# Decay tables by powers on GpSimd instead of exponentials on ScalarE, in a fused retention and gated feed-forward kernel

## The chip, the cores and the metric

The kernel runs on one core of a Trainium2 chip. The core has a matrix engine (TensorE, "PE" in the profile, with its weight loads as "PEld"), VectorE ("DVE"), ScalarE ("ACT"), GpSimd ("POOL"), a sync engine that issues most of the DMAs ("SP"), and 16 DMA engines. Every engine works through its own queue in order; semaphores make one engine wait for another. The metric is the device time of one execution in microseconds; the table below gives three runs of it. Times inside the kernel are counted from the start of the profiled span.

## What is computed

The inputs q, k and v have 8 batches, 8 heads, 576 positions and 64 values a head. Each head has a decay factor, and each score is weighted by the decay to the power of the distance:

```python
scores = (1.0 / np.sqrt(D_)) * np.matmul(q, k.transpose(0, 1, 3, 2))
gamma = 1.0 - 2.0 ** (-5.0 - np.arange(H, dtype=np.float32))
rel = pos[:, None] - pos[None, :]
Dmat = np.where(rel >= 0, gamma[:, None, None] ** rel[None, :, :], 0.0)
attn = np.matmul(scores * Dmat, v)
x = attn.transpose(0, 2, 1, 3).reshape(B * S, H * D)       # 4608 x 512
out = (sigmoid(x @ w_gate) * (x @ w_val)) @ w_out          # d_ff = 1536
```

There is no softmax, so the weight gamma to the power (i - j) can be split: q at position i is multiplied by gamma to the power i, and k (or v) at position j by gamma to the power -j. The kernel does so with two small tables, `qtab` (which also holds the scale of one over the root of 64) and `ktab`.

## The kernel before, in words

All of the work is written out in one program order, and each engine's queue follows that order; nothing reorders it at run time.

The first 512 positions of batch 0 and the first 256 of batch 1 are taken in three "pairs" of 256 positions (`load_pair`, `cast_pair`); everything else in "steps" of 128 positions (`load`, `cast_qk`, `cast_v`). For a pair, q, k and v arrive in f32 in six pieces. A piece of k is multiplied by the table `ktab2` on GpSimd (`kp`, L412), a piece of q by `qtab2` on VectorE (`qp`, L412); v is only cast to bf16 on GpSimd (`vp`, L409). TensorE then transposes kp and qp (`kTp`, `qTp`, L466), ScalarE copies the transposes out of PSUM (`kT`, `qT`, L476), TensorE computes scores (`qkp`, L485), VectorE multiplies them with the causal mask `trip` (`ptp`, L492), and TensorE multiplies them with v (`pvp`, L600) and sums up states (`st`, L522). Between these small groups the program puts matmuls on zeros (`fill`, L242, tile `idle`), ten at the very start and ten more between the first transposes and scores.

The outcome, transposed, is `xT`, and the feed-forward part takes it from there: gate and value matmuls (`hg`, `hv`, L1343 and L1408 for the first 512 rows, L885 and L1015 for later blocks), Sigmoid on ScalarE, a product on VectorE or GpSimd, and the output matmuls (`op`, L1502 and L1275). The weights arrive in f32 too, and are cast to bf16 in pieces (`cast_w`, L309), the first ones on GpSimd behind the kp and vp of the first two pairs. The loads of q, k, v of the first pairs and of the weights are all issued by the sync engine in one order (two half pieces by ScalarE), into 18 landing buffers (twelve called "ld" and six called "gsum"), which are used again in turn, so that the nineteenth load needs the first buffer free.

The decay tables are made at the very start, by `tables`, which is called twice: for the pairs with a tile of 128 x 2 x 8 x 2 (32 columns), and for the steps with one of 128 x 5 x 8 x 1 (40 columns). Each call makes an iota of positions `pos` on GpSimd (L252), multiplies it by the logarithm of each head's decay into `arg` (eight small VectorE instructions, L260), and takes two exponentials on ScalarE (L261 and L262). Between the calls stands the identity for the transposes (GpSimd, masks.py); the second call also corrects the positions of the last chunk on VectorE (L273). Then come a warm-up Sigmoid on ScalarE (L279), four VectorE memsets `sbd` (L285), and the mask `trip` on GpSimd (L288 and L290). Only behind these stand the first kp on GpSimd and the first qp on VectorE. Exp and Sigmoid each need a table of functions to be loaded on ScalarE (ACT_TABLE_LOAD in the profile); all later functions of the kernel are Sigmoid and copies.

Of the kernel before, what the change touches and what calls it, by code (L numbers as in the profile page):

```python
# [9 lines left out]
FP32 = mybir.dt.float32  # L10
BF16 = mybir.dt.bfloat16
AF = mybir.ActivationFunctionType
ALU = mybir.AluOpType
# [3 lines left out]
def kernel(  # L17
# [19 lines left out]
    nc = tc.nc  # L37

    B, H, S, D = q.shape
    NT, DM = out.shape  # L40
    DFF = moe_w_gate.shape[1]
    P = 128
# [13 lines left out]
    consts = ctx.enter_context(tc.tile_pool(name="consts", bufs=1))  # L56
# [192 lines left out]
    def tables(shape, pattern, step, put, fix=None):  # L249

        pos = consts.tile([P, pattern[0][1], pattern[1][1]], FP32, name=f"pos{step}")
        nc.gpsimd.iota(pos, pattern=pattern, base=0, channel_multiplier=step,  # L252
                       allow_small_or_imprecise_dtypes=True)
        if fix:
            fix(pos)
        arg = consts.tile(shape, FP32, name=f"arg{step}")
        qt = consts.tile(shape, FP32, name=f"qtab{step}")
        kt = consts.tile(shape, FP32, name=f"ktab{step}")
        for h in range(H):
            nc.vector.tensor_scalar_mul(put(arg, h), pos, math.log(1.0 - 2.0 ** (-5.0 - h)))  # L260
        nc.scalar.activation(out=kt, in_=arg, func=AF.Exp, bias=0.0, scale=-1.0)  # L261
        nc.scalar.activation(out=qt, in_=arg, func=AF.Exp, bias=lnscale, scale=1.0)  # L262
        return qt, kt

    lnscale = consts.tile([P, 1], FP32)
    nc.vector.memset(lnscale, math.log(1.0 / math.sqrt(D)))
    qtab2, ktab2 = tables([P, 2, H, 2], [[2 * P, 2], [1, 2]], 2, lambda t, h: t[:, :, h, :])
    ident = consts.tile([P, P], BF16)
    make_identity(nc, ident)


    def last_chunks(pos):
        nc.vector.tensor_scalar_add(pos[half(1), LAST], pos[half(1), LAST], -64.0)  # L273

    qtab, ktab = tables([P, NC, H, 1], [[P, NC], [1, 1]], 1, lambda t, h: t[:, :, h, :], last_chunks)
    qtab = qtab.rearrange("p c h o -> p c (h o)")
    ktab = ktab.rearrange("p c h o -> p c (h o)")
    warm = consts.tile([P, 1], FP32)
    nc.scalar.activation(out=warm, in_=lnscale, func=AF.Sigmoid)  # L279


    sbd = [lead.tile([P, M, P], BF16, name="sbd0")]
# [6 lines left out]
    for p0 in (0, 64):  # L289
        nc.gpsimd.affine_select(out=trip[p0:p0 + 64], in_=trip[p0:p0 + 64], compare_op=ALU.is_ge, fill=0.0,  # L290
                                base=0, pattern=[[-1, 2], [1, P]], channel_multiplier=-2)
# [1353 lines left out]
```

## Time and profile before

| | |
|---|---|
| median of three runs | 303.89 us (303.36 to 305.87) |
| the profiled execution | 304.38 us, of which 302.6 us are the span from its first to its last instruction |
| busy, share of the span: PE | 295.0 us, 97% |
| PEld | 249.9 us, 83% |
| DVE | 229.4 us, 76% |
| ACT | 204.5 us, 68% |
| POOL | 223.1 us, 74% |
| mean granted clock of TensorE | 0.998 |
| ACT_TABLE_LOAD | two, of 1.28 us each, at 1.89 and 3.98 us |

How to read it: the share of an engine's busy time says how full it is over the whole span, while the chain that ended last, followed back from the last instruction, says which engine's work or wait set the end. A row of the timeline gives start, length, engine, line, operation, the tile written and the tiles read, the shape and the count, and in square brackets how long the engine had been idle before it and what ended that. A row of the groups gives, behind the first bar, busy time in us and the mean of one in ns, and behind the second the idle time before them. A matmul's own busy time includes time in which neighbours overlap, so an almost full PE is not PE at its peak.

### The profile page before, as it was taken

What the parts mean: (1) busy time and instruction counts of PE and PEld (TensorE: products, weight loads), DVE (VectorE), ACT (ScalarE), POOL (GpSimd) and SP (SyncE); (2) the same over time, 40 slices, a digit from 0 to 9 for tenths busy, and PEclk for the clock granted to TensorE, in tenths of its full rate; (3) what the DMA queues carried; (4) which work ended last, traced back from release to release, by engine and by line L of the source; (5) the groups of instructions that cost most, each with busy time, mean ns of one, the idle gap of its engine ahead of it and who ended that gap; (6) DMA issues with size and microseconds to landing.
All of it is one profiled execution on the core that took longest, in us unless ns stands there. A gap on an engine that the chain in (4) does not pass through costs nothing.

```text
span 302.6 us, 10687 instructions
## 1 busy us (share of the span) xinstructions
PE 295.0 (97%) x4430; PEld 249.9 (83%) x4437; DVE 229.4 (76%) x433; ACT 204.5 (68%) x413; POOL 223.1 (74%) x250
## 2 busy tenths in 40 slices
PE   7899999999999999999999999999999999999994
PEld 3677785978868888888888888888888888888883
DVE  5958676786888998889848984896489948945893
ACT  6755574335359657985798589857985698559830
POOL 5775544755679888978997899689968946860780
PEclk9999999999999999999999999999999999999999
DMA  7999999979979999999749966976694155004013
GB/s 209 309 371 388 342 326 233 199 146 204 215 172 202 233 190 229 205 198 252 131 111 198 263 144 146 213 197 144 115 207 138 37 123 193 4 2 140 3 35 104
DMA packets 146464, 54.99 MB, mean 182 GB/s; under 512 B 124400, under 2 KB 139760, under 8 KB 146416
## 3 DMA queue, kind: packets, MB, share of 16 engines
q1 hardware_dynamic: 145328, 53.59, 72.7%
q10 hardware_dynamic: 1088, 0.72, 0.8%
q8 instruction: 34, 0.56, 0.8%
q14 instruction: 14, 0.11, 0.1%
HBM read 37.75 MB, written 9.44 MB: 156 GB/s over the span
## 4 chain that ended last, share of the span: by engine, by line
PE 95%; DMA 2%; ACT 1%; issue 0%; POOL 0%; SPq 0%; DVE 0%
PE gatea L1015 12%; PE wa L1015 12%; PE qa L1142 11%; PE qe L1142 9%; PE gatee L1015 6%; PE we L1015 6%; PE h_v L885 4%; PE h_g L885 3%; PE op L1275 3%; PE op L1502 3%; PE gateg L1015 3%; PE wg L1015 3%; PE hg L1343 3%; PE hv L1343 3%; PE val L717 2%; PE qa L1218 2%
## 5 line engine op out<-in xcount | busy, mean ns | idle before, releaser
L1015 PEld LDWEIGHTS <-wg_sb 128*128 128x128 bf16 x336 | 32.9, 98 | 4.0
L1042 POOL TENSOR_TENSOR gv<-gv,wu 128x512 bf16<-128x512 bf16 x20 | 23.4, 1172 | 15.6 <-DVE wu L1054 15.5
L1142 PEld LDWEIGHTS <-gsum 128*128 128x128 bf16 x312 | 30.0, 98 | 3.9 <-POOL xsum L969 0.2
L429 POOL TENSOR_TENSOR qk<-q,qtab 128x512 bf16<-128x512 f32 x28 | 30.3, 1082 | 3.5 <-DMA q<-in_q_dram 3.5
L1015 PEld LDWEIGHTS <-wv_sb 128*128 128x128 bf16 x296 | 29.0, 98 | 3.4
L942 POOL TENSOR_TENSOR gsum<-gsum,gv 128x256 bf16<-128x256 bf16 (+1 forms) x20 | 17.6, 890 | 14.4 <-DVE gsum L942 12.6
L1054 DVE TENSOR_TENSOR gu<-gatee,gu 128x512 f32<-128x512 f32 x21 | 14.5, 690 | 18.0 <-ACT gateg L1046 7.5
L1015 PEld LDWEIGHTS <-wgt_sb 128*128 128x128 bf16 x252 | 24.7, 98 | 2.9
L1015 PE MATMUL gatea<-xsum,wg_sb 128*128 128x256 bf16 x168 | 25.0, 273 | 0.0
L1142 PEld LDWEIGHTS <-gv 128*128 128x128 bf16 x228 | 21.8, 98 | 2.7
L942 POOL TENSOR_TENSOR gsum<-gv,gsum 128x256 bf16<-128x256 bf16 (+1 forms) x24 | 21.9, 920 | 0.2
L703 DVE TENSOR_TENSOR pt<-row,tri 128x512 bf16<-128x512 f32 x30 | 19.2, 680 | 3.1 <-PE row L686 2.7
L429 POOL TENSOR_TENSOR qk<-k,ktab 128x512 bf16<-128x512 f32 x11 | 11.6, 1056 | 13.0 <-DMA k<-in_k_dram 10.2
L1057 DVE TENSOR_TENSOR gs<-gatea,gs 128x512 f32<-128x512 f32 x21 | 14.5, 689 | 8.8 <-PE gatea L1015 8.6
L442 POOL TENSOR_TENSOR v<-v,ktab 128x512 bf16<-128x512 f32 x19 | 20.7, 1090 | 0.0
L1015 PE MATMUL wa<-xsum,wv_sb 128*128 128x256 bf16 x136 | 20.4, 273 | 0.0
L658 ACT CAST sb<-s 128x512 bf16<-128x512 f32 (+1 forms) x26 | 14.4, 568 | 8.5 <-DVE s L828 8.4
L787 ACT CAST xT<-val 128x512 bf16<-128x512 f32 x26 | 14.7, 592 | 6.9 <-PE val L733 6.9
L942 DVE TENSOR_TENSOR gsum<-gv 128x512 bf16<-128x512 bf16 (+1 forms) x34 | 18.8, 580 | 0.0
L1015 PEld LDWEIGHTS <-wvt 128*128 128x128 bf16 x168 | 16.4, 98 | 1.9
L942 POOL TENSOR_TENSOR gsum<-gv 128x256 bf16<-128x256 bf16 (+1 forms) x20 | 17.6, 881 | 0.0
L1042 POOL TENSOR_TENSOR gv<-gv,ws 128x512 bf16<-128x512 bf16 x14 | 16.3, 1164 | 1.0 <-DVE ws L1057 1.0
(203 smaller groups left out, 879.4 us busy)
## 6 DMA issues: line engine op xcount, KB each, us to landing
k<-in_k_dram SPq DMA_DIRECT2D x26, 256.0 KB, 3.9
q<-in_q_dram SPq DMA_DIRECT2D x26, 256.0 KB, 4.2
v<-in_v_dram SPq DMA_DIRECT2D x26, 256.0 KB, 4.7
out_dram<-ob SPq DMA_DIRECT2D x24, 256.0 KB, 3.2
wg<-in_moe_w_gate_dram SPq DMA_DIRECT2D x12, 256.0 KB, 5.4
wv<-in_moe_w_val_dram SPq DMA_DIRECT2D x12, 256.0 KB, 5.4
wo<-in_moe_w_out_dram SPq DMA_DIRECT2D x12, 256.0 KB, 5.4
v32p<-in_v_dram SPq DMA_DIRECT2D x6, 256.0 KB, 4.5
```

Source lines behind the costliest of these rows:

```text
L429: eng.tensor_tensor(out=to, in0=by_halves(loaded[s][1 - i]), in1=tab, op=ALU.mult)
L442: nc.gpsimd.tensor_tensor(out=natural["v", s], in0=loaded[s][2], in1=tab, op=ALU.mult)
L703: nc.vector.tensor_tensor(out=t[:, y, 0:n].rearrange("p i m t -> p (i m) t"), in0=rows_tile[ss[0]][y][:, 0:n].rearrange("p i m t -> p (i m ...
L787: nc.scalar.copy(out=to, in_=src)
L885: nc.tensor.matmul(ps[:, i], lhsT=w_sb[:, kc, (fc + i) * P:(fc + i + 1) * P], rhs=xT(kc, slice(t0, t0 + n)), start=(kc == 0), stop=(kc == ...
L942: eng.tensor_tensor(out=to, in0=a, in1=b, op=op)
L1015: nc.tensor.matmul(ps[:, f], lhsT=w[:, kc, f * P:(f + 1) * P], rhs=x[:, kc], start=(first and f == 0 and kc == 0), stop=(f == 1 and kc == ...
L1042: eng.tensor_tensor(out=to, in0=to, in1=src[:, part], op=ALU.mult)
L1054: nc.vector.tensor_tensor(out=me["u2"], in0=e, in1=me["u2"], op=ALU.add)
L1057: nc.vector.tensor_tensor(out=me["s5"], in0=a, in1=me["s5"], op=ALU.add)
L1142: nc.tensor.matmul(ps[:, b], lhsT=left(fp)[:, b * P:(b + 1) * P], rhs=right(fp), start=(first and fp == 0 and b == 0), stop=(fp == NFC // ...
L1343: nc.tensor.matmul(ps[:, cols], lhsT=(wg_sb if what == "g" else wv_sb)[:, kc, fc * P:(fc + 1) * P], rhs=xT(kc, cols), start=(kc == 0), sto ...
```

## The change

The tables are made without logarithm and exponential. A tile `decay` of 128 x 8 holds each head's decay (eight VectorE memsets of one column). Each call of `tables` makes a negated copy `back` of the positions on VectorE, and then GpSimd raises the decay to the power of `back` (into `ktab`) and of `pos` (into `qtab`), with both operands broadcast to the table's shape. VectorE then multiplies `qtab` by the scale. The tile `arg`, its 16 multiplies and `lnscale` go, and so do the four exponentials on ScalarE; the warm-up Sigmoid takes its input from a VectorE memset of its own. Program order stays: first table, identity, second table, warm-up, `sbd`, `trip`.

```diff
@@ in tables(shape, pattern, step, put, fix=None) @@
-        arg = consts.tile(shape, FP32, name=f"arg{step}")
         qt = consts.tile(shape, FP32, name=f"qtab{step}")
         kt = consts.tile(shape, FP32, name=f"ktab{step}")
-        for h in range(H):
-            nc.vector.tensor_scalar_mul(put(arg, h), pos, math.log(1.0 - 2.0 ** (-5.0 - h)))
-        nc.scalar.activation(out=kt, in_=arg, func=AF.Exp, bias=0.0, scale=-1.0)
-        nc.scalar.activation(out=qt, in_=arg, func=AF.Exp, bias=lnscale, scale=1.0)
+        back = consts.tile([P, pattern[0][1], pattern[1][1]], FP32, name=f"back{step}")
+        nc.vector.tensor_scalar_mul(back, pos, -1.0)
+        base = decay.unsqueeze(1).unsqueeze(3).to_broadcast(shape)
+        for t, to in ((back, kt), (pos, qt)):
+            nc.gpsimd.tensor_tensor(out=to, in0=base, in1=t.unsqueeze(2).to_broadcast(shape), op=ALU.pow)
+        nc.vector.tensor_scalar_mul(qt, qt, 1.0 / math.sqrt(D))
         return qt, kt
 
-    lnscale = consts.tile([P, 1], FP32)
-    nc.vector.memset(lnscale, math.log(1.0 / math.sqrt(D)))
+    decay = consts.tile([P, H], FP32)
+    for h in range(H):
+        nc.vector.memset(decay[:, h:h + 1], 1.0 - 2.0 ** (-5.0 - h))
...
     warm = consts.tile([P, 1], FP32)
-    nc.scalar.activation(out=warm, in_=lnscale, func=AF.Sigmoid)
+    nc.vector.memset(warm, 0.0)
+    nc.scalar.activation(out=warm, in_=warm, func=AF.Sigmoid)
```

## The prediction

> **What bounds the kernel now.** I read the page's busy times and its chain first, then the stretches, and then the first 18 us, where the change lies. The first row gives each engine's busy time (share of the span) and instructions, the second the shares of the chain that ended last.
>
> ```profile
> PE 295.0 (97%) x4430; PEld 249.9 (83%) x4437; DVE 229.4 (76%) x433; ACT 204.5 (68%) x413; POOL 223.1 (74%) x250
> ...
> PE 95%; DMA 2%; ACT 1%; issue 0%; POOL 0%; SPq 0%; DVE 0%
> ```
>
> TensorE is nearly the whole chain. Next, stretches of the span: length, then busy time (and instructions) of PE, PEld, DVE, ACT and POOL, then granted clock, DMA share and GB/s.
>
> ```profile
> 17.00:19.00 2.00, 1.51 (x15) 1.12 (x15) 1.10 (x2) 0.49 (x2) 1.45 (x3) 1.00 1.09 382
> ...
> 21.00:40.00 19.00, 18.95 (x160) 14.99 (x160) 14.57 (x26) 10.85 (x20) 11.30 (x18) 1.00 1.05 358
> 40.00:50.00 10.00, 9.79 (x164) 6.97 (x164) 6.99 (x13) 5.90 (x12) 4.50 (x6) 1.00 1.05 289
> 50.00:150.00 100.00, 99.73 (x1690) 84.52 (x1693) 83.31 (x152) 63.47 (x128) 78.62 (x81) 1.00 0.93 198
> 150.00:250.00 100.00, 100.00 (x1572) 89.09 (x1570) 73.84 (x138) 80.09 (x165) 84.60 (x90) 1.00 0.71 159
> 250.00:295.00 45.00, 45.00 (x570) 39.88 (x569) 33.70 (x59) 30.93 (x66) 29.83 (x29) 1.00 0.19 60
> ```
>
> From 21 to 295 us PE idles 0.05 + 0.21 + 0.27 + 0 + 0 = 0.53 us. So whatever the start of the kernel loses by 21 us reaches the end almost whole; only the 0.49 us idle between 17 and 19 us and those 0.53 us could swallow any of it. Now the start, by the chain in order of time:
>
> ```profile
> 1.84 4.91 DMA k32p<-in_k_dram
> ...
> 6.81 1.05 POOL kp L412
> ...
> 7.91 0.40 PE kTp L466 x4
> ...
> 8.74 0.24 PE qTp L466 x4
> ...
> 9.00 0.74 ACT qT L476
> ...
> 9.78 0.42 PE qkp L485 x16
> ```
>
> Until 6.74 us the chain is a load: the second piece of k. ScalarE's exponentials and its table loads, all before that, are not in it.
>
> **What the change removes.** ScalarE's rows of the timeline (start, length, line, what):
>
> ```profile
> 1.89 1.28 ACT L261 ACT_TABLE_LOAD   x1 [1.89 <-issue]
> 3.18 0.23 ACT L261 ACTIVATE ktab<-arg 128x32 f32<-128x32 f32 x1
> ...
> 3.98 1.28 ACT L279 ACT_TABLE_LOAD   x1
> 5.28 0.20 ACT L279 ACTIVATE warm<-lnscale 128x1 f32<-128x1 f32 x1
> 5.53 0.59 ACT L476 COPY kT<-kTp 128x512 bf16<-128x512 bf16 x1
> ```
>
> One load of 1.28 us and the four exponentials (3.18 to 3.98, between the two loads) go: 2.08 us of ScalarE. What is it worth? ScalarE's first useful work is the copy at 5.53, which needs a transpose of kp; qp follows, and its q lands only at 4.6 us (row of 4.65 below). GpSimd did wait for the tables, 1.00 us, so kp could begin up to 1.0 us sooner; but then the second k at 6.74 is what comes late, as now. I cost the gain at 0, with 1.0 as its other end.
>
> **What the change adds.** The rows of GpSimd and VectorE:
>
> ```profile
> 0.90 0.14 POOL L252 IOTA pos<- 128x4 f32 x1 [0.39 <-POOLq L1629]
> 0.99 0.20 POOL masks.py:197 MEMSET ident<- 128x128 bf16 x1
> 1.27 0.34 POOL masks.py:199 TENSOR_SCALAR_AFFINE_SELECT ident<-ident 128x128 bf16<-128x128 bf16 x1
> 1.57 0.16 POOL L252 IOTA pos<- 128x5 f32 x1
> 1.68 0.34 POOL L288 MEMSET trip<- 128x256 bf16 x1
> 2.10 0.90 POOL L290 TENSOR_SCALAR_AFFINE_SELECT trip<-trip 64x256 bf16<-64x256 bf16 x2
> 4.00 1.04 POOL L412 TENSOR_TENSOR kp<-k32p,ktab 128x512 bf16<-128x512 f32 x1 [1.00 <-ACT qtab L262]
> ...
> 17.42 0.61 POOL L309 CAST wg_sb<-wg 128x512 bf16<-128x512 f32 x1 [1.50 <-DMA wg<-in_moe_w_gate_dram]
> ```
>
> ```profile
> 0.94 0.06 DVE L266 MEMSET lnscale<- 128x1 f32 x1
> 1.08 0.97 DVE L260 TENSOR_SCALAR arg<-pos 128x4 f32<-128x4 f32 x8
> 2.08 0.15 DVE L273 TENSOR_SCALAR pos<-pos 64x1 f32<-64x1 f32 x1
> ...
> 3.23 1.09 DVE L285 MEMSET sbd<- 128x256 uint32 x4
> 4.65 0.93 DVE L412 TENSOR_TENSOR qp<-q32p,qtab 128x512 bf16<-128x512 f32 x1 [0.33 <-DMA q32p<-in_q_dram]
> 7.51 0.89 DVE L412 TENSOR_TENSOR qp<-q32p,qtab 128x512 bf16<-128x512 f32 x1 [1.93 <-DMA q32p<-in_q_dram]
> ```
>
> GpSimd gets four powers, two of 128x32 and two of 128x40: 144 columns. In program order they stand ahead of the identity, the second iota and the causal mask (`trip`), so all of these move behind powers, and the first kp behind all. No row shows a power on any engine. The nearest rows are GpSimd's two-operand products and differences:
>
> ```profile
> L942 POOL TENSOR_TENSOR gsum<-gsum,gv 128x512 bf16<-128x512 bf16 x8 | 9.5, 1191 | 6.9 <-DVE gsum L942 6.9
> L942 POOL TENSOR_TENSOR gsum<-gsum,gv 128x256 bf16<-128x256 bf16 x12 | 8.0, 689 | 7.5 <-DVE gsum L942 5.7 <-PE gatea L1015 1.5 <-ACT glance L752 0.3
> ```
>
> (1191 - 689) / 256 = 1.96 ns a column, and 187 ns that don't depend on columns. **From below**: a power as cheap as one such pass gives 4 x 0.187 + 144 x 0.00196 = 1.0 us for all four; with the iota's 0.14 us for each, 0.6. **From above** no row stops it. A power must be put together from a logarithm, a product and an exponential: two polynomials of some 7 steps, taking exponents apart and putting them together, and the special cases; my estimate is 28 passes of 1.96 ns, 55 ns a column, and the far end of the same kind three times that. Chosen: 144 x 0.055 + 4 x 0.187 = **8.65 us** (call it W); ends 0.6 and 24. I stay in the middle, since ScalarE's short time for an exponential comes with a table that it has to load, and GpSimd shows no such load.
>
> The Trainium skill (GPSIMD Engine Reference, section 7, Performance pitfalls for Q7 kernels) says that a chain of dependent fp32 steps costs 4 cycles each on this engine, and section 1 gives 1.2 GHz; for 28 steps that would be 93 ns a column, W = 14.2 us, and by the sum below some 318 us. No run here shows it.
>
> Now the path to the first kp, in which VectorE takes part. Eight memsets (0.06 each, in place of `lnscale`) run from 0.94 to 1.42. The negated positions `back` follow, priced like the correction at 2.08 (0.15): 1.57, and with a handoff of 0.05 us (as from the warm-up's end at 5.48 to the copy) the first power begins at 1.62. Then the powers, W = 8.65; between the second and third the identity, 0.99 to 1.61 above, 0.62; the second iota 0.16, VectorE's correction of it 0.15 and its `back` 0.15, with three handoffs 0.61; after the fourth the mask, 1.68 to 3.00 above, 1.32. First kp: 1.62 + 8.65 + 0.62 + 0.61 + 1.32 = **12.8 us**, against 4.00. VectorE gets to qp at the same time: behind the fourth power it still has the scaling of `qtab` (0.15), a memset (0.06) and the 1.09 us of `sbd`, all queued behind its wait. ScalarE's warm-up now waits for a VectorE memset too, but its kT copy is not due until 1.5 us after kp. The 16 small multiplies that go (0.97 us twice) were hidden behind ScalarE's table load, and give nothing now.
>
> **What hides part of it.** All early loads will have landed, so the second kp follows the first at once, at 13.9 rather than 6.81: 7.1 late, not 8.8. But VectorE, PE and ScalarE then go through their queues in order. From the first kp (4.00) to the first score matmuls took
>
> ```profile
> 6.86 0.42 PE L485 MATMUL qkp<-qT,kT 64*64 64x128 bf16 x16 [0.17 <-ACT qT L476]
> ```
>
> 2.86 us, so these come at 15.7. Behind them on PE lie, in order, their own 0.42, the second kTp (0.40), two fillers (2 x 0.27, from 0.81 for three below) and qTp (0.24), and then ScalarE's qT copy of 0.74: the second score matmuls come at 18.0, against 9.78: **8.2 late**. From there both orders run alike, since before, too, PE, ScalarE and VectorE were in the chain and not DMA. GpSimd catches up (its wait of 1.50 us for a weight at 17.42 goes), so it isn't late for the weights. Later slack takes up to 1.0 us back. Against this, PE may run slow when it starts again. The ten filler matmuls at the start take twice as long each as the later three:
>
> ```profile
> 1.05 3.90 PE L242 MATMUL idle<-blank 128*128 128x512 bf16 x10 [1.05 <-DVE blank L229]
> ...
> 5.88 0.81 PE L242 MATMUL idle<-blank 128*128 128x512 bf16 x3
> ```
>
> After 4.95 PE would stand idle for 9 us. If it falls back to that pace, three plus two fillers in the chain and the transposes between cost some 1.3 us more. I let these two cancel. Loads: the eighteen landing buffers are first reused here:
>
> ```profile
> 14.37 0.91 SPq L199 DMA_DIRECT2D wv<-in_moe_w_val_dram  x2
> ```
>
> The first kp would be done at 13.9, before that issue, so the loads aren't held up; with longer powers they would be, by no more than the work that needs them.
>
> **Sum**: 304.38 us of the profiled execution (302.6 of span and 1.8 around it) + 8.2 = **312.6 us**. Against the median of the runs, 303.89, it would be 312.1. In general the loss is about W - 0.4: every microsecond of powers beyond the first 0.4 is lost.
>
> **Rivals.**
> 1. *Not slower: powers as cheap as products.* The decision lies in one price: up to W = 0.4 the first loads cover everything, and up to W = 3.4 (about 18 ns a column, nine passes) the loss stays under 3.04 us, 1% of the time, which is about what a measurement of this kernel can tell from no change. At W = 1.0 the time is 304.4 + 0.6 = 305.0. For it: these tables are small. Against it: nine passes are few for a logarithm and an exponential.
> 2. *Code for the power has to be fetched at its first use.* The time then comes in one lump ahead of the first power. The only instruction fetches in the profile are in
>
> ```profile
> q8 instruction: 34, 0.56, 0.8%
> ```
>
> which names no user, so I bound the lump by what the first GpSimd wait of this kind shows below (0.39 us ahead of the first iota) and by the 4.91 us of the slowest early load in the chain above; with the latter 312.6 + 4.9 = 317.5 us. The instruction order of the changed kernel has no extra instruction ahead of the powers. The skill (GPSIMD Engine Reference, section 2.1, Instruction dispatch) gives about 6 us for the first call of freshly loaded code, which would make it 318.6.
> 3. *Partitions in turn.* If GpSimd could not do its partitions together in a power, each that it takes in turn costs the column price again: with ten in turn 144 x 0.55 + 0.75 = 80 us, and 384 us; with all 128 a thousand. No row of GpSimd looks like that; each is a few ns a column.
> 4. *Faster.* ScalarE's 2.08 us would have to be on the path with the powers nearly free. The most there is, is GpSimd's wait of 1.0 us: 303.4, which still is no change.
>
> **How the numbers follow.** Forecast (W from 3.4 to 24, 307.4 to 328): 0.60. Rival 1: 0.21. Rival 2: 0.06. Rival 3 or anything beyond 328: 0.11. Rival 4: 0.02. The range runs from 304 (rival 1 with nearly free powers) to 328 (W = 24), leaving out rival 3 and the faster end. Faster by over 1%: 0.01; within 1%: rivals 1 and 4, 0.22; slower: 0.77.
>
> **What the profile after will show.** Four TENSOR_TENSOR rows on GpSimd at L262 of the changed file; their length is W, and decides among the cases. A gap between the first iota and the first power of over 1 us says rival 2. First kp near 4.2 + W; second kp right behind it without a DMA wait; a PE gap from 4.95 to about a microsecond after the first kp; one ACT_TABLE_LOAD before 4 us. From 25 us on the order and the gaps as before, moved by a constant. If kp is late by W but the end isn't, slack after 21 us that the stretches don't show was there, and my reading of PE as the bound is wrong.

## The result, and the profile after

The changed kernel takes 331.25 us (median of four runs, 330.76 to 331.99), the kernel before 303.92 (four runs on the same chip, 303.36 to 305.87): a ratio of 1.0889, with a 95% interval from 1.0836 to 1.0941. It loses 27.3 us. The forecast was 312.6 us with a range up to 328, so the sign was right, and the size was outside the range.

The profiled execution took 331.33 us, 329.6 of them span. First the page's busy times, and the shares of the chain by engine and by line:

```profile
PE 297.3 (90%) x4430; PEld 250.9 (76%) x4437; DVE 227.8 (69%) x429; ACT 201.9 (61%) x408; POOL 248.3 (75%) x254
...
PE 87%; POOL 8%; DVE 2%; issue 1%; POOLq 0%; DVEq 0%
```

PE is busy for 2.3 us more than before, in a span that is 27 us longer. GpSimd has 25.2 us more of work, and has become 8% of the chain, from nothing; 8% of 329.6 is about 26 us. Here are rows of the changed kernel's timeline: GpSimd's powers, ScalarE's one table load, the first kp, the sync engine's first load behind it, and TensorE's first matmuls.

```profile
1.35 5.43 POOL L262 TENSOR_TENSOR ktab<-decay,back 128x32 f32<-128x32 f32 x1 [0.31 <-DVE back L259]
...
1.88 1.28 ACT L282 ACT_TABLE_LOAD   x1 [1.88 <-issue]
...
6.75 5.42 POOL L262 TENSOR_TENSOR qtab<-decay,pos 128x32 f32<-128x32 f32 x1
...
13.29 6.75 POOL L262 TENSOR_TENSOR ktab<-decay,back 128x40 f32<-128x40 f32 x1 [0.47 <-DVE back L259]
20.00 6.74 POOL L262 TENSOR_TENSOR qtab<-decay,pos 128x40 f32<-128x40 f32 x1
...
28.02 4.93 POOL L415 TENSOR_TENSOR kp<-k32p,ktab 128x512 bf16<-128x512 f32 x4
29.53 1.82 SPq L199 DMA_DIRECT2D wv<-in_moe_w_val_dram  x2
...
30.38 1.49 PE L242 MATMUL idle<-blank 128*128 128x512 bf16 x3
...
31.80 0.64 PE L488 MATMUL qkp<-qT,kT 64*64 64x128 bf16 x16
...
35.24 0.42 PE L488 MATMUL qkp<-qT,kT 64*64 64x128 bf16 x16
```

The four powers are 5.43 + 5.42 + 6.75 + 6.74 = 24.34 us, where I had put 8.65. Eight columns more cost 1.32 us more, so 165 ns a column between these two sizes. The first kp begins at 28.02 instead of 4.00, 24.02 late. The first power waited 0.31 us, for `back`, and there is one table load. TensorE's share of this is in its waits (us in total, times, longest):

```profile
PE kTp L469 <- POOL kp L415: 24.6, 1, 24.6
...
PE h_g L888 <- DVE gv L893: 0.9, 1, 0.9
```

One wait of 24.6 us. And the stretches, first of the start and then those that were shown of before (same columns: length, busy time and instructions of PE, PEld, DVE, ACT and POOL, clock, DMA share, GB/s):

```profile
20.00:25.00 5.00, 0.00 (x0) 0.00 (x0) 0.00 (x0) 0.00 (x0) 5.00 (x2) 0.50 0.00 0
25.00:30.00 5.00, 0.44 (x5) 0.45 (x6) 3.22 (x8) 0.20 (x1) 4.79 (x6) 0.50 0.00 0
30.00:35.00 5.00, 5.00 (x38) 2.53 (x36) 2.09 (x4) 2.50 (x4) 5.00 (x6) 0.51 0.63 182
...
50.00:150.00 100.00, 98.66 (x1515) 80.35 (x1521) 79.52 (x143) 56.44 (x111) 64.54 (x69) 1.00 0.89 202
150.00:250.00 100.00, 100.00 (x1570) 88.89 (x1568) 75.49 (x142) 80.86 (x166) 87.59 (x93) 1.00 0.83 180
```

Three things are to be seen. From 20 to 25 us GpSimd alone works. The clock granted to TensorE is 0.50 while it stands idle, and still 0.51 in the five microseconds in which its work begins again. And from 20 to 30 us no byte moves: all eighteen landing buffers are full, and the sync engine's next load stands until the first kp has freed a buffer, at 29.53. Behind 50 us PE is as full as before, but for 1.34 us of idle time between 50 and 150 (0.27 before).

So the 27.0 us of span are taken apart by following the same instruction in both traces (before, then after):

| instruction | before | after | late by | added here |
|---|---|---|---|---|
| first kp | 4.00 | 28.02 | 24.02 | 24.02 |
| first score matmuls | 6.86 | 31.80 | 24.94 | 0.92 |
| second score matmuls | 9.78 | 35.24 | 25.46 | 0.52 |
| first hg | 15.63 | 41.11 | 25.48 | 0.02 |
| score matmuls of a step, at 62.29 before | 62.29 | 88.25 | 25.96 | 0.48 |
| the same of a later step | 109.75 | 136.81 | 27.06 | 1.10 |
| end of the span | 302.6 | 329.6 | 27.0 | -0.06 |

The 0.48 is a gap in the chain behind the first hg with no releaser in either trace, 0.53 us long before and 1.01 after (first the chain of before, then of the changed kernel):

```profile
16.96 0.53 issue
```

```profile
42.44 1.01 issue
```

The packets in the traces show more of such gaps. Queue q8 brings instructions in packets of 16 KB, 34 of them in both kernels, and 35 in the two kernels below in which TensorE alone got more matmuls. A packet starts at 15.15 us before and at 41.20 after, and TensorE goes on 2.3 and 2.2 us behind that. In all the traces of this document TensorE stands eleven times for over 0.5 us without a releaser; ten of these gaps end 2.2 to 2.4 us behind the start of such a packet, and one 2.9. So TensorE has probably run out of instructions there. No run tests this, and what sets the start of a packet stays open.

Of the 1.10, 0.9 is the wait of h_g in the waits above; the last section comes back to it.

### The profile page after: what moved, and what is told of

Same layout as the page of the kernel before. It is cut to its first block, busy times and chain, and to the rows that moved or that the text cites. A ratio compares the mean times of both kernels' runs of the same rounds, so it can differ in the third digit from the quotient of the medians.

```text
span 329.6 us, 10679 instructions
## 1 busy us (share of the span) xinstructions
PE 297.3 (90%) x4430; PEld 250.9 (76%) x4437; DVE 227.8 (69%) x429; ACT 201.9 (61%) x408; POOL 248.3 (75%) x254
## 4 chain that ended last, share of the span: by engine, by line
PE 87%; POOL 8%; DVE 2%; issue 1%; POOLq 0%; DVEq 0%
PE gatea L1018 11%; PE wa L1018 11%; PE qa L1145 10%; PE qe L1145 8%; PE gatee L1018 6%; PE we L1018 5%; POOL ktab L262 4%; POOL qtab L262 4%; PE op L1278 3%; PE op L1505 3%; PE gateg L1018 3%; PE wg L1018 3%; PE hg L1346 3%; PE hv L1346 3%; PE h_v L888 2%; PE h_g L888 2%
## 5 line engine op out<-in xcount | busy, mean ns | idle before, releaser
L469 PE MATMUL kTp<-ident,kp 128*128 128x128 bf16 x24 | 2.8, 249 | 24.6 <-POOL kp L415 24.6
L1145 PEld LDWEIGHTS <-gv 128*128 128x128 bf16 x228 | 21.8, 98 | 2.9 <-issue 0.2
L432 POOL TENSOR_TENSOR qk<-k,ktab 128x512 bf16<-128x512 f32 x11 | 12.9, 1169 | 13.7 <-DMA k<-in_k_dram 7.7
L945 POOL TENSOR_TENSOR gsum<-gv,gsum 128x256 bf16<-128x256 bf16 (+1 forms) x24 | 21.8, 919 | 0.2
L469 PEld LDWEIGHTS <-kp 128*128 128x128 bf16 x24 | 1.8, 108 | 25.9 <-POOL kp L415 25.1
```

The costliest lines, as they stand in the source:

```text
L432: eng.tensor_tensor(out=to, in0=by_halves(loaded[s][1 - i]), in1=tab, op=ALU.mult)
L945: eng.tensor_tensor(out=to, in0=a, in1=b, op=op)
L1145: nc.tensor.matmul(ps[:, b], lhsT=left(fp)[:, b * P:(b + 1) * P], rhs=right(fp), start=(first and fp == 0 and b == 0), stop=(fp == NFC // ...
```

## Experiments

Each kernel was timed against the kernel before on the same chip. The question of the first three was whether the length of the powers is the whole loss; of the next one, what sets their price; of the others, what the remaining 2.7 us are, and whether a delay on GpSimd hurts wherever it stands.

### A product instead of the power

All instructions, waits and places stay. The tables hold decay times position, so the output isn't the reference's.

```diff
-            nc.gpsimd.tensor_tensor(out=to, in0=base, in1=..., op=ALU.pow)
+            nc.gpsimd.tensor_tensor(out=to, in0=base, in1=..., op=ALU.mult)
```

> The changed kernel with a product in each place of a power (so the tables hold decay times position, not the decay's powers; all else, the order and the waits too, is as in the changed kernel). Theory A, the length of the powers alone is the loss: four products of some 0.2 to 0.3 us, first kp at about 5 us, time within 1 us of the kernel before, 304 to 305. Rival B, the new order and the waits between VectorE and GpSimd cost by themselves: over 306.

Measured: 305.52 us (304.82 to 306.12) against 304.06, ratio 1.0041 [1.002, 1.0063]. From its timeline:

```profile
1.36 0.24 POOL L262 TENSOR_TENSOR ktab<-decay,back 128x32 f32<-128x32 f32 x1 [0.32 <-DVE back L259]
...
4.64 1.49 POOL L415 TENSOR_TENSOR kp<-k32p,ktab 128x512 bf16<-128x512 f32 x1
```

The first product is 0.24 us long where the power was 5.43, and the four are 1.0 together. The first kp comes 0.64 late, and of 27.3 us there remain 1.5. So the new order, the new waits and the four products cost 1.5 us together; the rest of the loss is the time of the powers. The prediction's first rival, with W = 1.0 and 305.0 us, is this kernel.

### TensorE kept busy meanwhile

The fillers at the start, 10 matmuls on zeros, become 120, so that TensorE works until the first kp.

```diff
-    FILLS = (0, 0, 10)
+    FILLS = (0, 0, 120)
```

> The changed kernel with 120 filler matmuls at the start in place of 10, so that TensorE stays busy until about 28.7 us, just before the first transposes. If the granted clock of 0.50 between 10 and 35 us costs something of its own, the matmuls of the start run at full pace and 0.9 to 1.4 us come back: about 330. If the extra loss behind the first kp comes from elsewhere, the time stays at 331.2.

Measured: 333.25 us (332.13 to 333.72), ratio 1.0929 [1.0883, 1.0974]; not less than the changed kernel's 331.25. The timeline, and the stretch in which work begins again:

```profile
30.03 0.81 PE L242 MATMUL idle<-blank 128*128 128x512 bf16 x3
31.27 0.42 PE L488 MATMUL qkp<-qT,kT 64*64 64x128 bf16 x16 [0.44 <-ACT qT L479]
33.50 0.42 PE L488 MATMUL qkp<-qT,kT 64*64 64x128 bf16 x16 [0.17 <-ACT qT L479]
39.46 0.61 PE L1411 MATMUL hg<-xT,wg_sb 128*128 128x256 bf16 x4
```

```profile
30.00:35.00 5.00, 4.39 (x64) 2.53 (x62) 3.25 (x6) 3.26 (x6) 5.00 (x6) 1.00 0.62 182
```

The clock is 1.00 in this stretch (0.51 in the changed kernel), the three fillers between the transposes and the scores take 0.81 us instead of 1.49, the second scores come 1.74 us sooner, and the first hg 1.65 us sooner (39.46 for 41.11). That is what the cold start costs in these two executions. But it doesn't reach the end. The chain of this kernel between 55 and 74 us runs through loads of the output weights and their casts:

```profile
68.07 4.03 DMA wo<-in_moe_w_out_dram
...
72.13 0.62 ACT wo_sb L317
72.74 0.28 ACT sb L654
...
73.95 4.45 PE op L1505 x13
```

A copy of states on ScalarE (`sb`) stands behind such a cast, and TensorE waits 2.29 us for it, until 73.07. The next output matmuls are then no earlier than in the changed kernel (73.95 for 73.99 us), whose chain holds no load there. And behind this wait TensorE is cold once more. The stretch shows it, and in the changed kernel's chain the same matmuls take 1.5 us less:

```profile
75.00:80.00 5.00, 5.00 (x29) 2.44 (x27) 3.10 (x8) 1.81 (x4) 2.29 (x3) 0.81 1.09 248
```

```profile
73.99 2.97 PE op L1505 x13
```

So TensorE, kept warm at the start, arrives ahead of its weights, waits for them, and pays for a cold start after all: at 75.5 us this kernel is 1.4 us behind the changed one. The 2.3 us at the end of the span also hold a gap of 0.82 us without a releaser at 261 us, while the changed kernel's wait of 0.9 us for h_g is missing here. These weights come last in the sync engine's order, behind the loads that stood until 29.5 us in both kernels; that they are late for this reason was not tried by itself.

### One power of 16 columns

The power is taken only of 128 x 16 (position within a chunk, for both signs); the tables come from it by VectorE products with constants, the table for the steps behind the first pairs.

```diff
+    nc.gpsimd.tensor_tensor(out=one, in0=decay, in1=pos.unsqueeze(2).to_broadcast([P, 2, H]), op=ALU.pow)
+    nc.vector.tensor_tensor(out=both, in0=one, in1=one, op=ALU.mult)
+    for i, t in ((1, ktab2), (0, qtab2)):
+        nc.vector.tensor_tensor(out=t, in0=two[i], in1=both[:, i]..., op=ALU.mult)
```

> One power of 16 columns only (decay and its inverse to the power of the partition number); the tables are products of it with constants on VectorE, those of the steps later. Theory A, 165 ns a column and 0.15 fixed: the power takes 2.8 us, first kp at about 4.8 us, time 304 to 305, no gain from the table load that is gone. Rival C, a lump at the first power whatever its size: the power or the gap ahead of it takes 5 us or more, time over 306. Rival D, the table load saved is worth something: below 303.

Measured: 308.59 us (307.92 to 309.21), ratio 1.0127 [1.0079, 1.0174].

```profile
1.54 2.91 POOL L256 TENSOR_TENSOR one<-decay,pos 128x16 f32<-128x16 f32 x1 [0.51 <-DVE decay L254]
...
6.25 2.41 POOL L425 TENSOR_TENSOR kp<-k32p,ktab 128x512 bf16<-128x512 f32 x2
```

My expectation was too low. It had overlooked that the identity and the mask still stand behind the power on GpSimd, so that the first kp is 2.25 us late; and by the end that has grown to 4.0 us of span. TensorE again stood idle from its first fillers until the transposes, and then worked at the pace of its start (the last section shows it). A small delay here costs more than itself.

### What a power costs

The kernel before, with powers on scratch tiles added behind its last work on GpSimd: other widths, other numbers of partitions, exponents all zero, and a product for comparison.

```diff
+    probe("t128x32", 128, 32)
+    probe("t128x1", 128, 1)
...
+    probe("t1x32", 1, 32)
+    probe("tzero", 128, 32, b=pz)
+    probe("tmult", 128, 32, op=ALU.mult)
+    probe("tlast", 128, 32)
```

> The kernel before with powers on a scratch tile behind all its work, which only make it longer: 128 partitions by 1, 8, 32 and 64 columns, 64, 32 and 1 partition by 32 columns, exponents all zero, and one product of 128 by 32. Theory A: 0.15 us plus 165 ns a column, so 0.3, 1.5, 5.4 and 10.7 us. If the partitions are worked on together, 64, 32 and 1 partition also take 5.4; if in turn, less in proportion. If the cost hangs on the exponent, zeros are cheaper. The product 0.2 to 0.3.

Measured: 347.25 us with the added work, which is of no interest. The groups of GpSimd, each shape apart (busy us, mean ns):

```profile
L1625 POOL TENSOR_TENSOR t128x<-scr 128x64 f32<-128x64 f32 x1 | 10.5, 10547 | 0.0
L1625 POOL TENSOR_TENSOR t128x<-scr 128x32 f32<-128x32 f32 x1 | 5.4, 5439 | 3.5 <-DVE scr L1620 3.5
...
L1625 POOL TENSOR_TENSOR tzero<-scr 128x32 f32<-128x32 f32 x1 | 5.4, 5419 | 0.0
...
L1625 POOL TENSOR_TENSOR t1x<-scr 1x32 f32<-1x32 f32 x1 | 5.4, 5417 | 0.0
L1625 POOL TENSOR_TENSOR tlast<-scr 128x32 f32<-128x32 f32 x1 | 5.4, 5417 | 0.0
...
L1625 POOL TENSOR_TENSOR t128x<-scr 128x1 f32<-128x1 f32 x1 | 0.6, 565 | 0.0
L1625 POOL TENSOR_TENSOR tmult<-scr 128x32 f32<-128x32 f32 x1 | 0.2, 242 | 0.0
```

From 1 to 64 columns, (10547 - 565) / 63 = 158 ns a column, and about 0.41 us that don't depend on columns; 40 columns by this are 6.75 us, as in the changed kernel. One partition costs what 128 cost, an exponent of zero what any other costs, and the first power is 22 ns longer than the last. This settles rivals 2 and 3: no code is fetched in a lump (the 6 us that the Trainium skill, GPSIMD Engine Reference, section 2.1, Instruction dispatch, gives for a first call show up in no run here), and the partitions aren't taken in turn. A power of 128 x 32 costs 22 products of the same shape.

### Powers for the first table only

The second table is made as before, by exponentials, and ScalarE loads two tables again. W is 10.85 us.

```diff
+        if step == 1:
+            return exp_tables(shape, pattern, step, put, fix)
```

> Powers for the first table only (two of 32 columns, 10.85 us); the second table by exponentials as in the kernel before. First kp at about 14.3 us, 10.3 later than before. If the loss is the delay of the first kp plus what a cold TensorE costs (about 1.5 us), 304.4 + 11.8, about 316. By the rule of the prediction (W - 0.4) 314.8. If the further loss seen in the changed kernel behind the start (1.6 us) comes with any delay, 317.5.

Measured: 317.6 us (316.98 to 319.28) against 304.27, ratio 1.0436 [1.0375, 1.0497]: 13.3 us for 10.85 of powers. The first kp is 10.13 late, the first hg 10.6 (26.25 for 15.63), the end of the span 12.7. That is 45% of the powers' time and 49% of the loss.

### The same with TensorE kept busy

```diff
-    FILLS = (0, 0, 10)
+    FILLS = (0, 0, 55)
```

> The same, with 55 filler matmuls at the start instead of 10, so that TensorE is busy until just before the first kp is ready. Here the landing buffers are given back before the sync engine needs them, so the loads are not held up. If the cold TensorE costs 1.5 us, this is 1.3 to 1.7 us faster than the kernel without the fillers; if not, the same.

Measured: 318.25 us (317.58 to 320.0), ratio 1.0457 [1.0383, 1.0531]; the intervals of this and the last kernel overlap. The first hg comes 0.86 us sooner (25.39 for 26.25), and at 62 us of before's time the kernel is 9.1 late instead of 11.0. The load that needs the first free buffer is issued at 15.19 us (14.37 before), so the loads are hardly held up. Between 140 and 200 us the kernel loses its gain again, in gaps of PE, the longest of them behind a copy of ScalarE (us in total, times, longest):

```profile
PE qa L1167 <- ACT xT L812: 1.4, 1, 1.4
```

I found no cause for this one. Two more have no releaser (0.60 us at 157 and 1.23 at 187 us), and are among those that end shortly behind a packet of instructions. So again the cold start can be seen, and again removing it doesn't shorten the kernel.

### Two sums moved in VectorE's queue

In the changed kernel VectorE is late for h_g at about 105 us, where sums of weight pieces stand ahead in its queue. Here two of them stand later.

```diff
-                "... 1.6:g12v ... 1.5:g02v ..."
+                "... 1.10:g12v ... 1.9:g02v ..."
```

> The changed kernel, with two of VectorE's weight sums in the second block of 256 rows moved four units later, since in its trace TensorE waits 0.9 us there for a product on VectorE that stands behind them. If that queue is the cause, the wait goes and the time falls by up to 1 us, to about 330.3; if it only moves, 331.2.

Measured: 331.3 us (329.77 to 332.58), ratio 1.0875 [1.0806, 1.0944]. In the profiled execution the wait is gone, and it took 329.77; but the median is that of the changed kernel. Most of that execution's advantage isn't the edit's: up to 90 us, ahead of the moved sums, it is already 1.3 us ahead of the changed kernel's profiled execution, with the second scores at 34.48 us instead of 35.24 and a gap of 0.53 behind the first hg instead of 1.01. At h_g it gains 0.95 us, and two thirds of that are lost again by 138 us. The wait is real where it occurs and about 1 us long, and the runs don't show that removing it helps.

### One power of 8 columns, nothing behind it

Identity and mask ahead of the power, the negative powers by VectorE's reciprocal, and VectorE's `sbd` memsets moved behind the first qp. The tables are those of the reference, and ScalarE loads one table of functions.

```diff
+    make_identity(nc, ident)
...
+    nc.gpsimd.tensor_tensor(out=one[:, 0], in0=decay, in1=pos.to_broadcast([P, H]), op=ALU.pow)
+    nc.vector.tensor_tensor(out=both[:, 0], in0=one[:, 0], in1=one[:, 0], op=ALU.mult)
+    nc.vector.reciprocal(out=both[:, 1], in_=both[:, 0])
```

> One power of 8 columns (1.46 us), behind the identity; squares, reciprocals and products with constants on VectorE make the tables. First kp at about 4.3 us, first qp before 5. If the length of the powers ahead of the first kp is the whole loss, 304 to 305, and nothing faster than the kernel before, though one table load is gone; if the freed ScalarE is worth something, below 303.

Measured: 304.58 us (303.9 to 306.61, ten runs) against 304.27, ratio 1.0001 [0.997, 1.0033]: no difference. The profiled execution was the longest of the ten.

```profile
1.51 1.65 POOL L257 TENSOR_TENSOR one<-decay,pos 128x8 f32<-128x8 f32 x1
1.87 1.28 ACT L291 ACT_TABLE_LOAD   x1 [1.87 <-issue]
4.45 1.04 POOL L423 TENSOR_TENSOR kp<-k32p,ktab 128x512 bf16<-128x512 f32 x1
```

With a power that costs 1.65 us the change does what it says, one table load and no exponentials, and gains nothing. The removed load was not on the path.

### Other work of GpSimd in place of the powers

Two memsets of a weight tile that is filled later, and a product, stand for each power. The tables hold products, so the output isn't the reference's.

```diff
+            for i in range(2):
+                nc.gpsimd.memset(spend[:, 0:2460 if step == 2 else 3080], 1.0)
-            nc.gpsimd.tensor_tensor(out=to, in0=base, in1=..., op=ALU.pow)
+            nc.gpsimd.tensor_tensor(out=to, in0=base, in1=..., op=ALU.mult)
```

> Each power is replaced by two memsets of other memory (2460 or 3080 columns of a weight tile that is filled later) and one product, so that GpSimd is busy about as long as with the powers, some 5.3 and 6.6 us for each, 23.5 us in all; the tables hold products of decay and position instead of powers. If only the length of the delay ahead of the first kp counts: first kp at about 27 us and a time of 328 to 332 us, like the changed kernel's 331. Rival, that the power instruction itself disturbs other engines while it runs (its reads, its port, its clock): clearly less than 328 us at the same first kp.

Measured: 326.29 us (324.35 to 326.86) against 304.51, ratio 1.0698 [1.0648, 1.0748].

```profile
0.99 4.35 POOL L266 MEMSET wt_sb<- 128x2460 bf16 x2
...
23.06 4.95 POOL L419 TENSOR_TENSOR kp<-k32p,ktab 128x512 bf16<-128x512 f32 x4
```

The memsets came out shorter than I had sized them (4.35 us for the first pair), so the first kp is at 23.06, not 27. From there the loss is the same kind: 19.06 late at the first kp, 19.98 at the first hg (35.61), 21.5 at the end of the span, 21.8 in the medians. The excess of the end over the first kp is 2.4 us, where powers give 3.0. So there is no sign that the power itself disturbs other engines; memsets in its place cost their delay and 2.4 us more too.

### The second table's powers later

These two stand behind the first pairs' kp and vp and the first weight casts on GpSimd.

```diff
-    qtab, ktab = tables([P, NC, H, 1], ..., last_chunks)
...
     def later_constants():
+        step_tables()
```

> Powers as in the change, but the second table's two (13.5 us) stand on GpSimd behind the kp and vp of the first pairs and the first weight casts, not ahead of the first kp. First kp at about 14 us (4.2 + 10.85 less the second iota's 0.5). If the 13.5 us are then hidden beside TensorE's work: about 317.5 us, like the kernel with powers for the first table only. If they hold back weight casts and step products that TensorE waits for: more, 318 to 324. If nothing is hidden wherever GpSimd stands still in the first 40 us: 331.

Measured: 335.45 us (334.42 to 336.24) against 304.51, ratio 1.0998 [1.095, 1.1047]: worse than the change, and worse than all three of my cases. The timeline:

```profile
37.45 6.75 POOL L262 TENSOR_TENSOR ktab<-decay,back 128x40 f32<-128x40 f32 x1 [12.08 <-DVE back L259]
...
52.33 3.59 PE L1351 MATMUL hv<-xT,wv_sb 128*128 128x512 bf16 x14 [15.89 <-POOL wv_sb L317]
```

The first kp comes at 14.38 as expected. But the iota of the second table hands its positions to VectorE, which has other work queued ahead of the correction and of `back`: GpSimd stands for 12.08 us, then raises powers for 13.5 us, and the weight casts behind them come so late that TensorE waits 15.89 us for one. To hide long work on GpSimd it would have had to stand behind these casts, and its inputs ahead; that wasn't tried.

### The loss against the delay

Kernels by how late the first kp is, in the profiled executions, and what becomes of it (us; the last column is the difference of the medians):

| kernel | powers or their stand-in | first kp late | span longer | median longer |
|---|---|---|---|---|
| product instead of power | 1.0 | 0.64 | 0.5 | 1.5 |
| one power of 16 columns | 2.9 | 2.25 | 4.0 | 4.5 |
| powers for the first table | 10.85 | 10.13 | 12.7 | 13.3 |
| memsets | 20.5 | 19.06 | 21.5 | 21.8 |
| the change | 24.34 | 24.02 | 27.0 | 27.3 |

From the third row to the last one, 13.9 us more of delay give 14.0 us more of time: one for one. All rows from the second on lie 1.8 to 3.3 us above the delay.

## Why the prediction was wrong in size

**The step that failed is the price of the power.** "Chosen: 144 x 0.055 + 4 x 0.187 = 8.65 us (call it W); ends 0.6 and 24." W was 24.34 us: 158 ns a column where I took 55, and 0.41 fixed where I took 0.19. That is a little beyond the far end of the range itself. The 28 passes were a guess at the steps of a power, and their price was the slope between two rows of another operation in bf16 (1.96 ns a column). The measured price is 80 such passes. A number that was put together from a guessed count of steps got a middle between ends 40 times apart, and the middle was taken because it was one. By the prediction's own rule (loss about W - 0.4) a W of 24.34 gives 328.3 us, so this term alone accounts for 15.7 of the 18.7 us of error. The Trainium skill's rule that I had set beside it (GPSIMD Engine Reference, section 7, Performance pitfalls for Q7 kernels: 4 cycles for each dependent fp32 step) gave an estimate of 93 ns a column with the same 28 steps, and 158 ns would be some 47 of them; it stood nearer to the measurement, and the count of steps is what neither had.

**The second failed step is "I let these two cancel"**: up to 1.0 us of slack given back against 1.3 us of cold TensorE. With W = 24.34 the second scores were to be 23.9 late and were 25.46. The first kp itself came 0.5 earlier than 4.2 + W; the first scores 3.78 us behind it instead of 2.86, the second 3.44 us behind those instead of 2.3. Of these 2.06 us, 1.74 go when TensorE is kept busy: the cold start is larger than my 1.3, and TensorE's clock was granted at 0.50 when work began. The Trainium skill says the same (TensorE: Matmul & The Clock Gate, Part 1: half the clock after an idle window of some 3.4 us). Shorter waits were enough here: behind 2.29 us, in the kernel with 120 fillers, the clock was 0.81 in the stretch from 75 to 80 us, and behind 1.78 us, in the kernel with the second table's powers later, 0.54 from 30 to 33. And no slack came back: 1.5 us more were lost behind the first hg, in the gap of 1.01 us and at h_g.

**"The loads aren't held up; with longer powers they would be, by no more than the work that needs them"** is half right. The sync engine stood until 29.53 and DMA at 0 from 20 to 30 us, as the sentence allows, and in the changed kernel no wait of TensorE on a load follows. But in the kernel with 120 fillers, weights are what TensorE waits for next.

**"From 25 us on the order and the gaps as before, moved by a constant"**: with W larger that would be from about 41 us on. It holds within 0.2 us from 106 us to the end, and not between 41 and 105, where 1.5 us are added.

What was right: the sign, and the path of it (powers ahead of identity, iota, mask and the first kp on GpSimd's queue; second kp right behind the first; PE as the bound after the start, so that a loss at the start reaches the end). The removed load and exponentials at 0 with an end of 1.0: the kernel with one power of 8 columns has them gone and is at 1.0001. Rival 1 was a true alternative, decided by the price alone, as the product instead of the power shows. Rivals 2 and 3 are out by the probe. What remains open: when TensorE's packets of instructions are fetched, if the gaps without releaser come from them, and why these come and go at other places when the start changes.

## What to carry to other kernels

An operation that the trace doesn't show, put on the path to the first work, is a price to be measured by itself, in a kernel of its own or at the end of this one, before the kernel is planned around it. The delay in front of a bound engine was lost whole here, with 1.8 to 3.3 us on top. Part of that is the cold start behind the wait; but keeping the engine warm only helps if what it needs next is there in time. What a removed instruction was worth is read from the chain: a table load and four exponentials beside a load of data were worth nothing, even when the replacement was nearly free.

## What the runs showed of the hardware

GpSimd's power took 0.41 us and 158 ns a column, for 1 partition or 128, for exponents of zero or not. A product of 128 x 32 took 0.24.

The clock column can mislead at the start of a trace. In the kernel with one power of 16 columns TensorE idles for 2.2 us, the column reads 1.00 in every stretch up to 40 us, and yet its three fillers are as long as in the changed kernel at 0.51. Its timeline, and the stretch in which they fall:

```profile
8.54 1.49 PE L242 MATMUL idle<-blank 128*128 128x512 bf16 x3
```

```profile
5.00:10.00 5.00, 2.79 (x17) 1.18 (x19) 2.92 (x9) 1.42 (x3) 4.63 (x6) 1.00 1.04 303
```

In this trace the records of the granted clock begin only at 13.39 us, with the full clock, and the column reads 1.00 where there is no record. In the kernel before they begin at 4.27 us. The durations fit: three fillers still take 1.40 us at 12.22, and the score matmuls at 13.54 take 0.42 again. So the durations of the fillers say more than the column here, and the half pace up to 13.4 us is the likely reason why 2.25 us at the first kp become 3.71 at the first hg (19.34 for 15.63).

The cold start doesn't cost the same each time. The records of the changed kernel return to the full clock at 34.95 us, and those of the kernel with two sums moved, which has the same program up to there and the same first transposes at 29.56, at 32.90; hence its second scores at 34.48 instead of 35.24. Between two stretches of full clock, half clock lasts whole multiples of 3.41 us in all these traces: 3.41, 10.24, 17.07, 20.48, 23.89 and 27.31 us.

VectorE's sums of bf16 pieces took more than twice as long at some places. The first fence is the changed kernel, where GpSimd's own bf16 sums run beside the first of these rows, and its f32 products of q and k beside the second; the next is the kernel before, with a cast on GpSimd:

```profile
100.46 1.15 POOL L368 TENSOR_TENSOR wgt_sb<-wg_sb,wgt_sb 128x512 bf16<-128x512 bf16 x1
100.80 1.08 DVE L327 TENSOR_TENSOR wt_sb<-wo_sb,wt_sb 128x512 bf16<-128x512 bf16 x1
...
102.86 1.22 POOL L432 TENSOR_TENSOR qk<-k,ktab 128x512 bf16<-128x512 f32 x1
103.10 2.44 DVE L368 TENSOR_TENSOR wg_sb<-wg_sb 128x512 bf16<-128x512 bf16 x2
```

```profile
74.78 0.42 DVE L324 TENSOR_TENSOR wt_sb<-wo_sb,wt_sb 128x512 bf16<-128x512 bf16 x1
...
76.62 0.80 POOL L444 CAST v<-v 128x512 bf16<-128x512 f32 x1 [0.52 <-PE h_g L885]
76.87 1.16 DVE L365 TENSOR_TENSOR wg_sb<-wg_sb 128x512 bf16<-128x512 bf16 x2
```

A single sum took 1.08 us beside GpSimd's, and 0.42 before; two took 2.44 instead of 1.16, and the product for h_g was queued behind them. That GpSimd's operands are the cause fits these rows and was not tested by itself. If it is, the shift of 24 us had brought the two engines' work together there, and so a delay at the start made a wait of 0.9 us at 105.
